# Eleven edits to the plan of a softmax-attention and spectral-filter kernel: first and last rounds, filler matmuls, first projection, last reciprocals

## The chip, the cores and the metric

The kernel runs on one core of one Trainium2 chip. The metric is the device time in microseconds of one execution, and the number to beat is the median of three runs. The engines named below are TensorE (PE, with its weight loads as PEld), VectorE (DVE), ScalarE (ACT), GpSimd (POOL) and SyncE (SP), which only issues transfers here.

## The reference, cut to what matters

A gate mixes two branches that read the same input `x` (2048 tokens of 448 channels): attention with 16 heads of 28 channels, and a filter in the Fourier domain.

```python
x = A_x                                                # [1, 2048, 448] bf16
g = sigmoid((x * gate_w).sum(-1, keepdims=True))
# a: attention
q, k, v = split_heads(x @ wqkv)                        # 16 heads, 28 channels each
p = softmax(q @ k.T * 28 ** -0.5)
a = merge_heads(p @ v) @ wo
# b: spectral filter
X = rfft2(x) * (w_r + 1j * w_i)
b = irfft2(X, s=(2048, 448))
return g * a + (1 - g) * b
```

## The kernel before, in words

The program is not written in the order in which it runs. Each method of the class `Kernel` describes operations (an engine, a planned duration, what they depend on, a key that is a due time, an earliest time `rel`), and the class `Sched` plays them through a small model of the core (`Sched.run`, L237). At each moment each engine takes the ready operation with the lowest key; transfers have a fixed planned latency. The order in which the model starts the operations is then emitted and fixed: on the chip every engine works its own list from the front, and waits where the front is not ready.

**Rounds.** Heads are worked in four groups `g` of four heads, tokens of the queries in four blocks `c` of 512. A round is one pair (g, c); there are 16 (`plan_steps`, L558), in the order (0,0), (0,1) to (3,3). In a round 16 tiles of 128 keys (`kt`) meet the block of queries for each of the four heads. One (kt, head) is a unit: a matmul with 32 rows (28 channels and the two norm terms) gives 128 keys x 512 queries of scores in PSUM, ACT takes the exponential, and four units of a tile, a quad, go into a PV matmul group that sums in the bank `pv`, with a ones column for the softmax denominators.

**Exponentials on ACT.** Units go in steps of three and two (`psA` of three banks, `psB` of two). L1143 evicts a step with one ACTIVATE into `ring`, which has 28 slots. A slot is taken again only when the PV matmul that read its last content is done, and PV quads run in a fixed order (`self.elems`).

**Exponentials on DVE and POOL.** `ND` says how many key tiles of a round ("d tiles") go another way: a dunit (a score matmul into one of two spare banks `bg`), a DVE instruction per head that turns the score into the bits of a bf16 power (L1099), and three more copies with a phase added (L1111, POOL or DVE), which PV multiplies with four scaled copies of V (`vd`), so a d tile costs four quads. `ND = [1] + [3] * 15`: key tile 15 in the first round, tiles 13 to 15 in the others. The d quads are spread through a round's list, the first one after three quads (where n % 4 == 0) or one.

**Two spare banks.** Everything else that TensorE does goes through the banks `bg`, an item at a time: transposing x (`x_block`), the projections of q and k (`proj_group`, L850: four matmul steps, two DVE instructions, a square sum `sq`, a row of norms `nrow` L885 and transfers of it into rows of q or k), of v (`v_block`), the gate (`gate_item`, L1001), the FFT stages (`background`, planned between `TA` 40 and `TB` 360 us) and the output tiles.

**Start.** `prologue` (L595) loads constants and the first 512 tokens, transposes them, and projects k and q of group 0 twice each: once into `psA`, squared by ACT (L708), and once into `psB`, onto which a matmul adds the norm row; DVE and ACT then evict `psB` (L719, L724, L728).

**After a round.** `normalise` (L1232) copies `pv` to SBUF, sends the denominators by DMA into a 128x16 tile, takes reciprocals (L1261), multiplies with the gate on POOL (L1262), goes through DRAM to spread them over partitions (`rsc`, `Rb`) and multiplies on POOL (L1272). For group 3 four output tiles can follow: eight matmul steps, k = 0 to 3 the spectral branch, 4 to 6 the earlier head groups, 7 group 3. After the last round there are no transfers: an fp32 matmul of 512 columns spreads the denominators, DVE takes the reciprocal of 128x512 (L1249) and multiplies, and `last_tile` (L1313) adds the last four output tiles in the banks that the scores have left.

**Filler.** Where the planned share of PE's time that was busy in the last 3.4 us (`HAMW`) is under `HAMF` = 0.7 and there is a gap, the planner puts a matmul of zeros into it, of the full array and up to 256 columns (`filler`, L800).

**Order of a group's projections.** `attention` (L1030) gives groups 1 to 3 due times a few us before the start of round 4g-1, all eight projections close together, and `v_block` after them.

Of the kernel before, what the change touches and what calls it, by code (L numbers as in the profile page):

```python
# [50 lines left out]
def fft_consts():  # L51
# [54 lines left out]
    for ri, B in enumerate((Br, Bi)):  # L106
# [8 lines left out]
       "sel4": (386, 32), "self": (418, 256)}  # L115
CSTN = 674


def small_consts():
# [26 lines left out]
    put32("self", self_)  # L146
    return m


class Op:  # L150
    __slots__ = ("lk", "eng", "dur", "emit", "deps", "key", "rel", "mode", "acq", "free", "lat",
                 "start", "end", "name", "step", "n")

    def __init__(self, eng, dur, emit, deps, key, rel, mode, acq, free, lat, name):
        self.eng, self.dur, self.emit = eng, dur, emit
        self.deps = [d for d in deps if d is not None]
        self.key, self.rel, self.mode = key, rel, mode
        self.acq, self.free, self.lat, self.name = acq, free, lat, name
        self.start = self.end = None
        self.step = None  # L160
        self.lk = eng == "POOL"

# [7 lines left out]
SWITCH = 0.1  # L170
HAMW, HAMF = 3.4, 0.7
DUE_P = 4.0
SWP = 1.0


class Sched:
# [60 lines left out]
    def run(self, nbg_tiles, dunits, dfree):  # L237
# [37 lines left out]
        def share(t):  # L275
            a = t - HAMW
            while pebusy and pebusy[0][1] <= a:
                pebusy.pop(0)
            return sum(e - max(s, a) for s, e in pebusy) / HAMW

        def fill(t):
# [17 lines left out]
            o = Op("PE", n / 2400.0, lambda: self.filler(target, n), (), 0.0, 0.0, "full", None, None, None, "fill")  # L299
            o.start = t + (SWITCH if mode not in (None, "full") else 0.0)  # L300
            o.end = o.start + o.dur
            order.append(o)
            pebusy.append((o.start, o.end))
# [3 lines left out]
        def finish(o, t0, dur):  # L307
            nonlocal left
            if o.eng == "PE":
                pebusy.append((t0, t0 + dur))  # L310
# [15 lines left out]
        while left:  # L326
            progress = False
            for e in engs:
                if free[e] > t + 1e-9:
                    continue  # L330
                best = None
                for o in pend[e]:
# [26 lines left out]
                if best is None:  # L359
                    if e == "PE" and t > 8.0:  # L360
                        f = fill(t)
                        if f:
                            free[e], mode = f, "full"
                            progress = True
# [58 lines left out]
class Kernel:  # L423
    ND = [1] + [3] * 15
    RING = 28
    T0 = 10.0
    TA, TB = 40.0, 360.0
# [25 lines left out]
    def alloc(self):  # L453
# [41 lines left out]
        self.gb3 = T([P, 512], BF16, "gb3")  # L495
# [62 lines left out]
    def plan_steps(self):  # L558
        self.groups = [(g, c) for g in range(4) for c in range(4)]
# [35 lines left out]
    def prologue(self):  # L595
        nc, sc = self.nc, self.sc
        K0 = -5000.0
        self.d_cst = self.dma(self.cst[:], nc.inline_tensor(small_consts(), name="ccst").ap(), (), K0, eng="AQ",
                              dur=0.1, lat=2.6)
# [89 lines left out]
        sv = self.c("svec").bitcast(F32)  # L689
        for wi, w in enumerate("kq"):  # L690
            b1 = [self.psA[:, 0, :], self.psA[:, 1, :]][wi]
            b2 = [self.psB[:, 0, :], self.psB[:, 1, :]][wi]
            first = {}
            for rnd, bank in ((0, b1), (1, b2)):
                ops = []
                for c in range(4):
                    n = 128 if c < 3 else 65

                    def f(c=c, n=n, w=w, bank=bank, rnd=rnd):
                        self.mm(bank, self.wpad[w, 0][0:n, c, :], self.xT[0][0:n, c, :], c == 0,  # L700
                                rnd == 0 and c == 3)
                    ops.append(self.pe(512, f, [self.xev[0, c]] + self.wready[w, 0] + ops[-1:],
                                       K0 + 20 + c * .1 + wi + 2 * rnd))
                first[rnd] = ops[-1]
# [4 lines left out]
            sq = self.act(0.65, fs, (first[0], tl, self.xev[0, 1]), K0 + 30 + wi)  # L709

            def fm(b2=b2, w=w, o=o):
                self.mm(b2, self.c("sel" + w), self.sq[:, o:o + 512], False, True)
            m = self.pe(512, fm, (sq, first[1]), K0 + 40 + wi)
            self.last_sqmm = m
            dst = self.k[0] if w == "k" else self.q[0]
            evs = []
            if w == "k":
                def fe(b2=b2, dst=dst):
                    self.pin(nc.vector.tensor_scalar(out=dst[:, 0:512], in0=b2, scalar1=sv, scalar2=None,  # L719
                                                     op0=ALU.mult))  # L720
                evs.append(self.dve(0.61, fe, (m,), K0 + 50))
            else:
                def fe1(b2=b2, dst=dst):
                    self.pin(nc.vector.tensor_scalar(out=dst[:, 0:272], in0=b2[:, 0:272], scalar1=sv,  # L724
                                                     scalar2=None, op0=ALU.mult))

                def fe2(b2=b2, dst=dst):
                    self.pin(nc.scalar.activation(out=dst[:, 272:512], in_=b2[:, 272:512], func=ACT.Copy, scale=sv))  # L728
                evs.append(self.dve(0.37, fe1, (m,), K0 + 51))
                evs.append(self.act(0.4, fe2, (m,), K0 + 51))  # L730
            (self.kev if w == "k" else self.qev)[0, 0] = evs
# [68 lines left out]
    def filler(self, bank, n):  # L800
        if bank is None:
            self.mm(self.pv[:, 0:n], self.zero[:, 0:P], self.zero[:, 0:n], False, False)
        elif bank < 0:
            self.mm(self.pv[:, 0:n], self.zero[:, 0:P], self.zero[:, 0:n], True, True)
        else:
            self.mm(self.bgt[bank][:, 0:n], self.zero[:, 0:P], self.zero[:, 0:n], True, True)
# [43 lines left out]
    def proj_group(self, w, g, blocks, due, rel):  # L850
# [5 lines left out]
        for j, b in enumerate(blocks):  # L856
            it = Item()
            dd = due - 8 + 5.0 * (j + 1) / nb
# [94 lines left out]
    def v_block(self, g, b, due, wop, rel=0.0):  # L953
# [23 lines left out]
        if b == 3:  # L977
            lo = 4 - min(len(self.dk[4 * g + c]) for c in range(4))
# [22 lines left out]
    def gate_item(self, due):  # L1001
# [5 lines left out]
        b = self.dve(0.16, lambda: self.pin(nc.vector.reciprocal(out=self.glog[:], in_=self.ge[:])), (a,), due)  # L1007
        b = self.dve(0.09, lambda: self.pin(nc.vector.tensor_copy(out=self.gg[:, 0:NT], in_=self.glog[:])), (b,), due)
# [18 lines left out]
        self.gb3d = self.dma(self.gb3[:], at([[0, P], [1, 512]], 12 * P), (s,), due + 2, lat=6.0)  # L1027


    def attention(self):  # L1030
# [15 lines left out]
        for g in range(1, 4):  # L1046
            d0 = ts[4 * g - 1]
            self.proj_group("k", g, [0, 1, 2, 3], d0 - 6.0, d0 - 60.0)
            self.proj_group("q", g, [0, 1, 2, 3], d0 - 2.0, d0 - 60.0)
            wop = self.w_block(g, [0, 1, 2, 3], d0 + 5, d0 - 15)  # L1050
            for b in range(4):
                self.v_block(g, b, d0 + 6 + 4.0 * b, wop, d0 - 15)
# [19 lines left out]
        for n, kt in dlist:  # L1072
# [14 lines left out]
            for s in range(4):  # L1087
# [7 lines left out]
                m.n = s  # L1095
                self.dunit_ops.append(m)
# [28 lines left out]
        for i, st in enumerate(self.steps):  # L1125
# [13 lines left out]
            m.step, m.n = i, [u[2] for u in st]  # L1139
            u0, ug = self.unit_slot[st[0]]  # L1140
# [91 lines left out]
    def normalise(self, n, last):  # L1232
# [8 lines left out]
        if n == 15:  # L1241
# [3 lines left out]
            m = self.pe(2048, lambda: self.mm(self.psB[:, 1, :], self.c("self").bitcast(F32), pvs[:], True, True),  # L1245
                        [ev, self.lastexp[1]], kk)
            a = self.dve(0.66, lambda: self.pin(nc.vector.tensor_tensor(out=pvs[:], in0=pvs[:], in1=self.gb3[:],
                                                                        op=ALU.mult)), (m, self.gb3d), kk, lk=True)
# [270 lines left out]
```

## Time and profile before

| | |
|---|---|
| median of 3 runs | 463.16 us (461.95 to 469.37) |
| the profiled execution | 463.34 us |
| its span, first to last instruction | 461.6 us |
| PE busy | 413.2 us, 90% |
| ACT busy | 390.1 us, 85% |
| DVE busy | 301.0 us, 65% |
| POOL busy | 261.0 us, 57% |
| mean granted TensorE clock | 0.948 |

The profiled execution is 1.7 us longer than its span, which is what lies around the first and the last instruction. A row of a timeline is: start, duration, engine, line, operation, output<-input with shapes, count, and in brackets how long the engine sat idle before it and what released it. A row of a table of stretches is: from and to, length, then the busy time of each engine with its count of instructions, the granted TensorE clock (1.00 is full), and the share and rate of the DMA engines.

### The profile page before, as it was taken

Reading aid. Unit: us, or ns where it says so; the run is one execution under the profiler, and the core shown is the slowest. Engines: PE = TensorE matmul, PEld = TensorE weight load, DVE = VectorE, ACT = ScalarE, POOL = GpSimd, SP = SyncE. Lnnn points to the kernel's source line nnn. Section 1 sums busy time; section 2 is a strip of 40 time slices with the busy share of each in tenths; the row PEclk is TensorE's granted clock in tenths of the full one; section 3 lists DMA queues with packets and bytes.
Section 4 is the critical chain, followed back from the end, with each engine's and each line's share of the span. In section 5 each row is a group of like instructions: output and inputs, shape, how many; then the busy total and the mean of one; then the engine's idle time right before and its main releaser. Section 6 shows DMA issues by size and latency. Waiting matters only on the chain.

```text
span 461.6 us, 11773 instructions
## 1 busy us (share of the span) xinstructions
PE 413.2 (90%) x4854; PEld 148.8 (32%) x4855; DVE 301.0 (65%) x492; ACT 390.1 (85%) x352; POOL 261.0 (57%) x230
## 2 busy tenths in 40 slices
PE   7889799989998898999889889799999899999894
PEld 5444221223342212223343223123333233333251
DVE  1558836776857847776867788366867776656325
ACT  2680667999999889999999899599999999999910
POOL 6825630673292387693296775398189592491910
PEclk9999855999999969999999999589999999999999
DMA  8210031101012321121112212002120221111101
GB/s 224 57 42 9 2 89 41 31 5 34 19 40 55 75 63 33 45 53 24 45 35 47 70 47 67 18 18 57 30 62 22 65 72 45 62 36 37 32 23 60
DMA packets 31586, 21.78 MB, mean 47 GB/s; under 512 B 16692, under 2 KB 29228, under 8 KB 31532
## 3 DMA queue, kind: packets, MB, share of 16 engines
q1 hardware_dynamic: 30140, 20.43, 17.2%
q8 instruction: 38, 0.62, 0.6%
q10 hardware_dynamic: 1392, 0.60, 0.5%
q14 instruction: 16, 0.13, 0.1%
HBM read 15.11 MB, written 1.97 MB: 37 GB/s over the span
## 4 chain that ended last, share of the span: by engine, by line
PE 38%; ACT 29%; DVE 9%; issue 8%; DMA 6%; SPq 6%; POOL 4%; ACTq 0%; POOLq 0%; DVEq 0%
ACT ring L1143 28%; PE bg L552 16%; PE pvb L552 10%; PE psA L552 7%; SPq L527 6%; PE psB L552 5%; POOL pd L1111 2%; DMA Rb<-rsc 2%; DMA X<-in_A_wqkv_dram 2%; DVE pd L1099 2%; DMA rsc<-rrg 1%; DVE pd L1111 1%; POOL q L1272 1%; DVE Rb L1249 1%; DVE vd L995 1%
## 5 line engine op out<-in xcount | busy, mean ns | idle before, releaser
L1143 ACT ACTIVATE ring<-psA 128x1536 bf16<-128x1536 f32 x168 | 260.4, 1550 | 17.6 <-PE psA L552 13.0
L1111 POOL TENSOR_SCALAR pd<-pd 128x2048 uint16<-128x2048 uint16 x105 | 197.4, 1902 | 80.3 <-DVE pd L1099 76.5
L1143 ACT ACTIVATE ring<-psB 128x1024 bf16<-128x1024 f32 x168 | 189.5, 1128 | 9.5 <-PE psB L552 8.9
L1099 DVE TENSOR_SCALAR pd<-bg 128x512 uint16<-128x512 f32 x184 | 122.4, 685 | 50.2 <-PE bg L552 38.3
L552 PEld LDWEIGHTS <-k 32*128 32x128 bf16 x1024 | 44.8, 91 | 151.3 <-issue 142.9
L552 PE MATMUL psA<-q,k 32*128 32x512 bf16 x504 | 70.2, 398 | 20.4 <-ACT ring L1143 16.5
L552 PE MATMUL pvb<-ring,vw 128*32 128x512 bf16 x840 | 84.7, 407 | 0.2
L552 PE MATMUL pvb<-pd,vd 128*32 128x512 bf16 x736 | 74.6, 401 | 4.9 <-POOL pd L1111 4.2
L552 PE MATMUL psB<-q,k 32*128 32x512 bf16 x336 | 70.4, 400 | 1.7 <-ACT ring L1143 1.2
L552 PE MATMUL bg<-q,k 32*128 32x512 bf16 x184 | 66.1, 396 | 2.8 <-DVE X L1366 1.4
L1272 POOL TENSOR_TENSOR q<-pvs,Rb 128x512 bf16<-128x512 f32 x15 | 19.2, 1282 | 32.8 <-DMA Rb<-rsc 17.2
L552 PEld LDWEIGHTS <-vw 128*32 128x32 bf16 x840 | 22.2, 97 | 26.6 <-issue 21.3
L552 PEld LDWEIGHTS <-vd 128*32 128x32 bf16 x736 | 19.9, 96 | 25.0 <-issue 20.1
L552 PEld LDWEIGHTS <-xT 128*32 128x32 bf16 (+3 forms) x512 | 20.1, 100 | 20.6 <-issue 17.7
L1111 DVE TENSOR_SCALAR pd<-pd 128x2048 uint16<-128x2048 uint16 x33 | 25.6, 798 | 0.2
L1423 DVE TENSOR_TENSOR t<-bg,Wg 128x450 bf16<-128x450 f32 x32 | 19.2, 618 | 7.2 <-PE bg L552 6.7
L552 PE MATMUL bg<-Bd,xT 128*32 128x450 bf16 (+1 forms) x256 | 20.4, 410 | 2.2 <-DVE X L1366 1.5
L864 DVE TENSOR_SCALAR q<-bg,cst 128x512 bf16<-128x512 f32 x15 | 11.3, 750 | 14.3 <-PE bg L552 14.3
L1309 DVE CAST fin<-bg 128x448 bf16<-128x448 f32 x12 | 7.5, 621 | 20.1 <-PE bg L552 20.1
L552 PE MATMUL bg<-xT,wpq 128*32 128x512 bf16 (+1 forms) x240 | 19.1, 399 | 0.0
L552 PE MATMUL bg<-xT,wpk 128*32 128x512 bf16 (+1 forms) x240 | 18.1, 387 | 0.5 <-DVE nrow L885 0.5
L1366 DVE CAST X<-bg 128x450 bf16<-128x450 f32 x16 | 9.9, 619 | 13.2 <-PE bg L552 13.2
(112 smaller groups left out, 366.1 us busy)
## 6 DMA issues: line engine op xcount, KB each, us to landing
Rb<-rsc SPq DMA_DIRECT2D x60, 64.0 KB
CS<-cCS SPq DMA_DIRECT2D x16, 192.0 KB
xtok<-Ab SPq DMA_DIRECT2D x16, 112.5 KB
Wg<-in_B_w_i_dram SPq DMA_DIRECT2D x64, 28.1 KB
V<-xtok SPq DMA_DIRECT2D x16, 112.5 KB
xtok<-in_A_x_dram SPq DMA_DIRECT2D x4, 448.0 KB
out_dram<-fin SPq DMA_DIRECT2D x12, 112.0 KB
Wg<-in_B_w_r_dram SPq DMA_DIRECT2D x32, 28.1 KB
```

Source lines behind the costliest of these rows:

```text
L527: self.pin(e.dma_start(out=out() if callable(out) else out, in_=in_() if callable(in_) else in_))
L552: self.pin(self.nc.tensor.matmul(out, lhsT=lhsT, rhs=rhs, start=start, stop=stop, **kw))
L864: self.pin(nc.vector.tensor_scalar(out=dst, in0=self.bgi(it), scalar1=self.sv, scalar2=None, op0=ALU.mult))
L995: self.pin(nc.vector.tensor_tensor(out=self.vd[g][:, f, :, :, 0:DH], in0=src, in1=wv, op=ALU.mult))
L1099: self.pin(nc.vector.tensor_scalar(out=ys[:, s, :].bitcast(U16), in0=self.bgi(it), scalar1=127 * UNITS, scalar2=0.0, op0=ALU.add, op1=ALU. ...
L1111: self.pin(e.tensor_scalar(out=fl(pds), in0=fl(ys), scalar1=float(PHASE[f]), scalar2=1.0, op0=ALU.add, op1=ALU.mult))
L1143: self.pin(nc.scalar.activation(out=self.ring[:, u0:u0 + len(st), :], in_=slot[:, 0:len(st), :], func=ACT.Exp, scale=LN2 / UNITS))
L1249: b = self.dve(0.66, lambda: self.pin(nc.vector.reciprocal(out=self.Rb[:], in_=self.psB[:, 1, :])), (m, self.rblast), kk)
L1272: e = self.pool(1.15, lambda: self.pin(nc.gpsimd.tensor_tensor(out=dst, in0=pvs[:], in1=self.Rb[:], op=ALU.mult)), ds, kk)
L1309: e = self.dve(0.55, lambda: self.pin(nc.vector.tensor_copy(out=fin[:], in_=self.bgi(it)[:, 0:D])), [ops[-1], self.fdma[t % 2]], key, free=it)
L1366: x1.append(self.dve(.54, lambda: self.pin(nc.vector.tensor_copy(out=self.X1[:, t, 0:F2], in_=self.bgi(it)[:, 0:F2])), ops[-1:] + pads, k, ...
L1423: self.pin(nc.vector.tensor_tensor(out=out[:], in0=self.bgi(it)[:, 0:F2].rearrange("p (a f) -> p a f", a=2), in1=free_dims(Wg[:], [[F, 2], ...
```

## The change

1. `ND[0]` goes from 1 to 0: in the first round all 16 key tiles go to ACT.
2. Filler: a matmul counts with a weight (`heat`), a quarter for each 32-row tile (dunit 0.25, score step 0.25 for each unit), 1 for all others; the bound `HAMF` goes from 0.7 to 0.5; a filler is four matmuls of 32 columns of weights each instead of one of 128.
3. A bank rule: an item that is no dunit may not take the last free `bg` bank while a ready dunit has a smaller key (`DUP`).
4. Constants are loaded in two parts (418 of 930 columns at the start; the rest, for the end, after planned time 60).
5. The first k and q are projected once. ACT squares the result, a matmul makes the norm rows in `psB`, ACT copies these to SBUF, and DVE adds them to the scaled projection.
6. The projections of groups 1 to 3 are spread: k and q get due times over a stretch from planned time 35, `ts[4]` or `ts[8]` to 16 us before the group's first round; v follows.
7. The order of the last eight rounds: (2,0), (2,1), (2,2), (3,0), (3,1), (3,2), (2,3), (3,3).
8. The rule "first d quad after three quads" holds for the first round of each group in that order.
9. After the last round: four small fp32 matmuls bring the denominators to a 128x16 tile, DVE takes the reciprocal and multiplies with the fp32 gate, copies it out to 128x512, four fp32 matmuls of 128 columns spread it into PSUM, and DVE multiplies.
10. The last output tiles: steps k = 0 to 6 get a late key (4000 + t instead of -30 + t), only k = 7 stays urgent.
11. The transfer of the gate's row (`gb3`) goes away.

```diff
-       "sel4": (386, 32), "self": (418, 256)}
-CSTN = 674
+       "sel4": (386, 32), "self": (418, 256), "idf": (674, 256)}
+CST1, CSTN = 418, 930
...
-HAMW, HAMF = 3.4, 0.7
+HAMW, HAMF = 3.4, 0.5
...
-            return sum(e - max(s, a) for s, e in pebusy) / HAMW
+            return sum((e - max(s, a)) * w for s, e, w in pebusy) / HAMW
...
+                        if ud is not None and o.name != "dunit" and len(bl) == 1 and ud < o.key + DUP:
+                            continue
...
-    ND = [1] + [3] * 15
+    ND = [0] + [3] * 15
+    PJE, PJV = 16.0, 16.0
...
-        self.groups = [(g, c) for g in range(4) for c in range(4)]
+        self.groups = ([(g, c) for g in range(2) for c in range(4)]
+                       + [(2, 0), (2, 1), (2, 2), (3, 0), (3, 1), (3, 2), (2, 3), (3, 3)])
...
+        for wi, w in enumerate("kq"):
+            b1, b2, o = self.psA[:, wi, :], self.psB[:, wi, :], 512 * wi
+            m = self.pe(512, lambda b2=b2, w=w, o=o: self.mm(b2, self.c("sel" + w), self.sq[:, o:o + 512], True, True),
+                        (sqs[w],), K0 + 40 + wi)
...
+            def fn(nr=nr, b2=b2):
+                self.pin(nc.scalar.copy(out=nr[:], in_=b2))
+            nn = self.act(0.5, fn, (m,), K0 + 45 + wi)
...
+                self.pin(nc.vector.scalar_tensor_tensor(out=dst[:, 0:512], in0=b1, scalar=sv, in1=nr[:],
+                                                        op0=ALU.mult, op1=ALU.add))
...
-            self.mm(self.bgt[bank][:, 0:n], self.zero[:, 0:P], self.zero[:, 0:n], True, True)
+        out = self.pv if bank is None or bank < 0 else self.bgt[bank]
+        self.mm4(out[:, 0:n], self.zero[:, 0:P], self.zero[:, 0:n], bank is not None, bank is not None)
...
-            dd = due - 8 + 5.0 * (j + 1) / nb
+            dd = due - 3 - spread * (nb - 1 - j) / nb
...
-            d0 = ts[4 * g - 1]
-            self.proj_group("k", g, [0, 1, 2, 3], d0 - 6.0, d0 - 60.0)
-            self.proj_group("q", g, [0, 1, 2, 3], d0 - 2.0, d0 - 60.0)
+            b0 = ts[self.fr[g]] - self.PJE
+            a0 = [0, 35.0, ts[4], ts[8]][g]
+            m0 = (a0 + b0) / 2
+            self.proj_group("k", g, [0, 1, 2, 3], m0, a0 - 10.0, m0 - a0)
+            self.proj_group("q", g, [0, 1, 2, 3], b0, a0 - 10.0, b0 - m0)
...
-            lo = 3 if n % 4 == 0 else 1
+            lo = 3 if n == self.fr[self.groups[n][0]] else 1
...
+                m.heat = 0.25
...
+            m.heat = 0.25 * len(st)
...
-            m = self.pe(2048, lambda: self.mm(self.psB[:, 1, :], self.c("self").bitcast(F32), pvs[:], True, True),
-                        [ev, self.lastexp[1]], kk)
...
-            b = self.dve(0.66, lambda: self.pin(nc.vector.reciprocal(out=self.Rb[:], in_=self.psB[:, 1, :])),
-                         (m, self.rblast), kk)
...
+                ms.append(self.pe(0, lambda j=j: self.mm(bank[:, 4 * j:4 * j + 4], pvs[:, 128 * j:128 * j + 128],
+                                                         self.c("self").bitcast(F32)[:, 0:128:32], True, True),
...
+            a = self.dve(0.2, lambda: self.pin(nc.vector.reciprocal(out=r[:], in_=bank[:, 0:16])), ms[-1:], kk)
...
+                ms2.append(self.pe(0, lambda j=j: self.mm(bank[:, 128 * j:128 * j + 128], self.Rx[:, j, :],
+                                                          self.c("idf").bitcast(F32), True, True),
...
+            x = self.dve(0.6, lambda: self.pin(nc.vector.tensor_copy(
+                out=self.Rx[:].rearrange("p j (s n) -> p j s n", n=32),
+                in_=free_dims(r2[:], [[4, 4], [1, 4], [0, 32]]))), (b,), kk)
...
+            e = self.dve(0.61, lambda: self.pin(nc.vector.tensor_tensor(out=dst, in0=pvs[:], in1=bank, op=ALU.mult)),
+                         ms2[-1:], kk)
...
-            o = self.pe(448, f, self.out_dep(t, k) + ops[-1:] + (self.lastexp if k == 0 else []), -30.0 + t, mode="col")
+            o = self.pe(448, f, self.out_dep(t, k) + ops[-1:] + (self.lastexp if k == 0 else []),
+                        -30.0 + t if k == 7 else 4000.0 + t, mode="col")
```

More of the change, by code (lines that the diff above doesn't have):

```diff
@@ L331, in run @@
                 best = None
+                ud = None
+                if e == "PE":
+                    for o in pend[e]:
+                        if o.name == "dunit" and rdy[o] <= t + 1e-9 and (ud is None or o.key < ud):
+                            ud = o.key
                 for o in pend[e]:
@@ L362, in run @@
                         if f:
-                            free[e], mode = f, "full"
+                            free[e], mode = f, "col"
                             progress = True
@@ L977, in v_block @@
         if b == 3:
[L978 removed]
+            lo = 4 - min(len(self.dk[self.nof[g, c]]) for c in range(4))
         vr = [wop[1]]
```

101 lines of the change are left out of this document (47 added, 54 removed).

## The prediction

> **What bounds the kernel now.** I read the page first (busy shares, then the 40 slices), then what ACT waited for, then the timelines of ACT and PE at the places where ACT's row is low.
>
> ```profile
> span 461.6 us, 11773 instructions
> PE 413.2 (90%) x4854; PEld 148.8 (32%) x4855; DVE 301.0 (65%) x492; ACT 390.1 (85%) x352; POOL 261.0 (57%) x230
> ACT  2680667999999889999999899599999999999910
> PEclk9999855999999969999999999589999999999999
> ```
>
> ACT's row is 9 almost everywhere between slices 7 and 38: the exponentials bound the middle. They are low at both ends, nil in slice 3, and low where the clock row reads 5 or 6. So I split the time into four terms: the head up to the first exponential, the exponentials back to back, ACT's waits between them, the tail.
>
> ```profile
> 15.32 1.45 ACT L1143 ACTIVATE ring<-psA 128x1536 bf16<-128x1536 f32 x1 [1.02 <-PE psA L552]
> ...
> 17.57 1.46 ACT L1143 ACTIVATE ring<-psA 128x1536 bf16<-128x1536 f32 x1
> ...
> 23.38 1.45 ACT L1143 ACTIVATE ring<-psA 128x1536 bf16<-128x1536 f32 x1 [1.10 <-PE psA L552]
> ...
> 31.56 1.12 ACT L1143 ACTIVATE ring<-psB 128x1024 bf16<-128x1024 f32 x1
> 39.21 0.18 ACT L933 ACTIVATE w<-bg 128x16 f32<-128x16 bf16 x1 [6.53 <-PE bg L555]
> 45.97 0.21 ACT L1003 ACTIVATE ge<-glog 128x16 f32<-128x16 f32 x1 [6.58 <-DVE glog L972]
> 48.27 1.45 ACT L1143 ACTIVATE ring<-psA 128x1536 bf16<-128x1536 f32 x1 [2.08 <-PE pvb L552]
> ...
> 438.79 1.03 ACT L1143 ACTIVATE ring<-psB 128x1024 bf16<-128x1024 f32 x1
> ```
>
> Head: 15.3. A pair of steps (five units) starts every 2.25 us (15.32 to 17.57), 0.45 a unit. The last exponential ends at 439.8, so the phase lasts 424.5 and the tail 461.6 - 439.8 = 21.8. ACT's waits between exponentials, by releaser:
>
> ```profile
> ACT ring L1143 <- PE psA L552: 13.0, 18, 1.6
> ACT ring L1143 <- PE psB L552: 8.9, 12, 2.8
> ACT ring L1143 <- PE bg L552: 2.9, 4, 1.1
> ACT ring L1143 <- PE pvb L552: 2.1, 1, 2.1
> ```
>
> Together 26.9, with the 6.53 and 6.58 of the two small ACTIVATEs above 40.0, less the 1.0 before the first exponential: 39.0. So 840 units take 424.5 - 39.0 = 385.5. Of the 39.0, 15.2 is one hole: nothing is evicted between 32.7 (31.56 + 1.12) and 48.27. By then 14 steps or 35 units are done, the ring holds 28, and only the first pair of quads (8 units) has been read: the second pair holds the first d quad of key tile 15, which waits for the last block of keys, its dunits and `vd`. The hole ends on a PV matmul. The other 23.8 lie mainly where the clock is halved:
>
> ```profile
> 50.00:80.00 30.00, 27.90 (x218) 6.18 (x214) 16.10 (x27) 20.40 (x18) 8.53 (x6) 0.60 0.21 50
> 160.00:180.00 20.00, 18.97 (x181) 4.83 (x179) 11.37 (x20) 17.59 (x16) 12.95 (x7) 0.74 0.20 52
> 280.00:310.00 30.00, 26.91 (x266) 7.42 (x265) 18.27 (x28) 23.75 (x21) 16.16 (x15) 0.77 0.14 34
> ```
>
> ACT is the fourth number with a count: idle 9.6 of the 30 us from 50, 2.4 of the 20 from 160, 6.2 of the 30 from 280, 18.2 in all. That leaves 23.8 - 18.2 = 5.6, of which 1.1 is the wait at 23.38.
>
> **First round on ACT (edits 1, 8).** It adds four units, 4 x 0.45 = 1.8 us, and takes four dunits, four DVE evictions, three phase copies and three PV quads net out of the first 50 us. The hole of 15.2 goes, since no PV quad of the first round waits for a d tile any more. What is late next is the second round's first d quad, which needs the same `vd` and the second block of queries. Its last DVE eviction before:
>
> ```profile
> 54.54 1.29 DVE L1099 TENSOR_SCALAR pd<-bg 128x512 uint16<-128x512 f32 x2 [0.27 <-PE bg L552]
> ```
>
> So at 55.8 even if nothing gets earlier, while ACT reaches round two at about 15 + 1.1 + 64 x 0.45 = 45 and has 28 slots, 12.6 us, in hand. So I count the hole as gone, and bound what comes in its place between 0 and 5 us: DVE must now do in 30 us, beside running exponentials, the projections that it did in the hole.
>
> **Filler, weights, bank rule (2, 3).** No row prices four-column fillers. There are 76 in this phase (55 and 21, rows below); if each held a score up by its pitch of 0.11 us (four in 0.61, each 0.28 long, so (0.61 - 0.28) / 3) that would be 8 us, if all lie in gaps, 0. They are put only where the plan has a gap and PE's matmuls leave 10% of the span open, so I take 0. The bank rule holds another item back by one dunit's eviction at most (0.65 by the row above, two in 1.29), and the spectral items that yield have until planned time 360: 0. What the fillers are worth is the clock:
>
> ```profile
> L552 PE MATMUL pvb<-zero x55: 230/282/394, 26.6 to 347.0; 128*128 128x256 bf16 x49, 128*128 128x128 bf16 x2, 128*128 128x192 bf16 x2, 128*128 128x224 bf16 x1
> L552 PE MATMUL bg<-zero x21: 272/273/283, 286.8 to 457.7; 128*128 128x256 bf16 x21
> ...
> 436.96 0.61 PE L552 MATMUL bg<-zero 128*128 128x256 bf16 x4
> ...
> 46.00:54.00 8.00, 5.10 (x66) 1.95 (x66) 7.96 (x13) 4.00 (x4) 5.62 (x3) 1.00 0.00 0
> 162.00:164.00 2.00, 1.46 (x11) 0.47 (x7) 1.78 (x4) 2.00 (x3) 0.21 (x1) 1.00 0.39 99
> 288.00:291.00 3.00, 0.50 (x5) 0.10 (x2) 0.00 (x0) 1.93 (x2) 3.00 (x3) 0.90 0.00 0
> ...
> 287.89 1.26 POOL L1272 TENSOR_TENSOR q<-pvs,Rb 128x512 bf16<-128x512 f32 x1 [5.13 <-DMA Rb<-rsc]
> ...
> 291.07 0.62 PE L552 MATMUL pvb<-pd,vd 128*32 128x512 bf16 x4 [2.56 <-POOL pd L1111]
> ```
>
> Each fall follows thin work. Before the first, DVE is full (7.96 of 8) and PE busy 5.10 of 8; the change lightens exactly that place. The second, at 164, comes with PE at work, mostly 32-row tiles: the weighted count sees it, the old one did not. The third is a surprise to any plan: POOL waits 5.13 for `Rb`, its next phase copy is late, PE stands 2.56. I take that one fall like the later two remains somewhere, (2.4 + 6.2) / 2 = 4.3, and bound it by 0 and 18.2.
>
> The Trainium skill, "TensorE: Matmul & The Clock Gate", section "Why this matters for your kernels", has the clock fall back after a matmul gap of about 3 us. The row of 288 to 291 agrees (2.56 idle), that of 162 to 164 does not (0.54 idle of 2, and it fell). By that rule alone the weighting would buy nothing at 164, and the sum would be 2.4 higher.
>
> **Single projection (4, 5).** It takes eight 512-column matmuls off PE and ACT's q eviction, and adds two ACT copies, which I price like the squares.
>
> ```profile
> 11.10 0.60 ACT L708 ACTIVATE sq<-psA 128x512 bf16<-128x512 f32 x1 [0.46 <-PE psA L552]
> ...
> 12.42 0.60 PE L552 MATMUL psB<-sq,cst 128*128 128x512 bf16 x2
> ...
> 13.05 0.75 DVE L719 TENSOR_SCALAR k<-psB,cst 128x512 bf16<-128x512 f32 x1 [4.35 <-DMA X<-in_A_wqkv_dram]
> ...
> 14.33 0.50 DVE L724 TENSOR_SCALAR q<-psB,cst 128x272 bf16<-128x272 f32 x1 [0.53 <-ACT q L728]
> ```
>
> The squares end at 11.7. Then: k copy 0.6, q norm matmul 0.4 (two take 0.60, the second begins 0.2 later), q copy 0.6, q add 0.75, and hops of 0.06 make 14.3, against 14.83 now, the end of the DVE part of q. First exponential at 14.8; bounds 14 (k and q overlap) and 15.8. The first wait, for the second key block (23.38), does not move, so it grows by the half microsecond: 1.6. The smaller constant load, the second one on SP's queue in mid-kernel and the missing `gb3` transfer touch queues on which no exponential waits here: 0.
>
> **Spread projections, order of rounds (6, 7).** The same instructions, moved. The SP and POOL queues see the same transfers in another order; of the 4.5 us of small waits left (5.6 - 1.1) I keep all, between 0 and 8. Group 3 starts a round earlier, but its keys' buffer is free from round 8, three rounds ahead. The gain of the order is in the tail: tiles 8 to 11 can be finished during rounds 14 and 15.
>
> **Tail (9, 10).** Now:
>
> ```profile
> 439.89 0.93 PE L552 MATMUL psA<-Bd,X 113*32 113x448 bf16 x16
> 440.65 0.74 PE L552 MATMUL psA<-wo,q 128*32 128x448 bf16 x12
> 441.22 0.93 PE L552 MATMUL psA<-Bd,X 113*32 113x448 bf16 x16
> ...
> 448.45 0.60 PE L552 MATMUL pvb<-ring,vw 128*32 128x512 bf16 x8
> 449.86 1.12 PE L552 MATMUL psB<-pvs,cst 128*128 128x512 f32 x2 [0.61 <-DVE pvs L1243]
> 451.63 3.35 DVE L1249 RECIPROCAL Rb<-psB 128x512 f32<-128x512 f32 x1
> 455.01 0.69 DVE L1251 TENSOR_TENSOR q<-pvs,Rb 128x512 bf16<-128x512 f32 x1
> ...
> L1261 DVE RECIPROCAL rr<-rs 128x16 f32<-128x16 f32 x15 | 3.6, 242 | 2.8 <-DMA rs<-pvs 2.8
> ```
>
> From 439.9 output steps run for 8.3 us ahead of the last PV group (ends 449.05); then 0.8 copy, 1.8 spreading, 3.35 reciprocal, 0.7 multiply, and 5.9 from 455.7 for the last step, the evictions and the transfer. After: PV first, its end about 1.0 after the last exponential; copy 0.8; four small matmuls; reciprocal 0.3; gate 0.25; copy out 0.7; four spreading matmuls; multiply 0.85; then 5.9. The small matmuls have no row: between 0.5 and 2.4, I take 1.3, near the 1.12 of the fp32 one; the spreading ones between 1.0 and 2.8, I take 1.8 (the same columns plus exposed weight loads). Sum 12.9. The steps k = 0 to 6 of four tiles (439.89 to 441.22 is one tile, 5.3 us of PE in all) no longer stand ahead, but only some 4 of it fits into the gaps: plus 1.3. Tail 14.2; bounds 12 and 16.7.
>
> **Sum.** Head 14.8 + exponentials 385.5 + 1.8 + waits (1.6 + 4.5 + 4.3 = 10.4) + tail 14.2 = 426.7, plus the 1.7 around the span: 428. That is against this execution's 463.3, which is the median (463.16) within 0.1.
>
> **Rivals.** (A) The waits stay: the hole goes, but the clock falls as long as before and DVE and the two banks, full early on, hold round two up. Waits 23.8 + 5, rest as above: 447. For it: 7.96 of 8 us of DVE before the first fall, and falls like the third that no filler sees. Against: PE gets scores and PV at the place where it was thin. The page's rule above belongs here.
>
> (B) The clock never falls and the waits shrink to the first one and some 2 us: 3.6, total 422. Against: one late `Rb` among 15 is enough.
>
> (C) The hole only moves: the second round's d quads stall the ring as the first did, 15.2 again with the old clock stretches: 14.8 + 387.3 + 39 + 14.2 + 1.7 = 457, no change to speak of. Against: three times as many key tiles pass before it.
>
> (D) Slower: the halved clock. In the 30 us from 50 ACT lost 9.6, of which by the mean clock some 24 halved: 0.40 lost per halved microsecond. If the narrow fillers do not hold the clock, it takes (463.3 - 428 + 9.3) / 0.40, about 112 us halved beyond what I counted, to be 2% slower. Against: the whole middle runs at 1.00 on narrow tiles.
>
> **Chances.** Mine (waits 6 to 18, 424 to 436) 0.55; A (436 to 454) 0.21; B 0.11; C 0.08; D 0.05. 2% is about what a measurement of this kernel can tell from no change: faster holds mine, A and B, 0.87; same C, 0.08; slower 0.05. The range reaches from 416 (B with no wait and a tail of 12) to 450 (A's upper part left out, with C and D).
>
> **What would show it.** Hole: no ACT wait over 3 us between 30 and 50. Head: first exponential before 15.3. Clock: the three fives of the clock row gone or fewer. Tail: last exponential to end about 14, no 3.35 reciprocal, the last PV group within 1.5 us of the last exponential. I am wrong if ACT stalls on PV in the second round, or if the clock row shows more fives.

## The result, and the profile after

| | before | after | predicted |
|---|---|---|---|
| median | 462.56 us (4 runs) | 436.63 us (4 runs, 435.51 to 438.8) | 428 (416 to 450) |
| ratio to before | | 0.9486, 95% interval 0.9384 to 0.9587 | |
| profiled execution, its span | 463.34, 461.6 | 438.8, 437.0 | |
| mean granted TensorE clock | 0.948 | 0.978 | |

Faster by 5.1%, inside the range. Medians take in all runs and ratios leave out those slowed by a low clock, from one of which the profile of before stems, so the two spans lie a little further apart than the ratio.

The page of the changed kernel, the same lines as before:

```profile
span 437.0 us, 11982 instructions
...
PE 390.3 (89%) x4956; PEld 145.9 (33%) x4957; DVE 295.3 (68%) x489; ACT 391.1 (89%) x355; POOL 254.9 (58%) x227
...
ACT  2888999998979999979997899999999999898970
...
PEclk9998999999999999988998989999999999999999
```

ACT is never nil in the middle now, and the clock row has no digit under 8. ACT's timeline, start, duration and in brackets the wait:

```profile
14.74 1.45 ACT L1150 ACTIVATE ring<-psA 128x1536 bf16<-128x1536 f32 x1 [1.27 <-PE psA L563]
...
23.66 1.45 ACT L1150 ACTIVATE ring<-psA 128x1536 bf16<-128x1536 f32 x1 [1.81 <-PE psA L563]
...
107.99 1.45 ACT L1150 ACTIVATE ring<-psA 128x1536 bf16<-128x1536 f32 x1 [1.30 <-PE pvb L563]
115.98 1.45 ACT L1150 ACTIVATE ring<-psA 128x1536 bf16<-128x1536 f32 x1 [0.86 <-PE pvb L563]
125.34 1.45 ACT L1150 ACTIVATE ring<-psA 128x1536 bf16<-128x1536 f32 x1 [2.48 <-PE pvb L563]
...
192.59 1.45 ACT L1150 ACTIVATE ring<-psA 128x1536 bf16<-128x1536 f32 x1 [1.35 <-PE psA L563]
...
236.93 1.02 ACT L1150 ACTIVATE ring<-psB 128x1024 bf16<-128x1024 f32 x1 [1.55 <-PE psB L563]
...
250.86 1.02 ACT L1150 ACTIVATE ring<-psB 128x1024 bf16<-128x1024 f32 x1 [1.12 <-PE pvb L563]
...
422.50 0.75 ACT L1150 ACTIVATE ring<-psB 128x512 bf16<-128x512 f32 x1
```

The hole of 32.7 to 48.3 is gone. What is new is an exponential that waits on PV, which means a full ring. By releaser (total us, times, longest):

```profile
ACT ring L1150 <- PE pvb L563: 11.4, 10, 2.5
ACT ring L1150 <- PE psA L563: 7.8, 9, 1.8
ACT ring L1150 <- PE bg L563: 2.8, 4, 1.1
ACT ring L1150 <- PE psB L563: 1.8, 2, 1.6
```

PV held ACT once for 2.1 us before, and at the end of the hole only; now ten times. PE does not stand still meanwhile. In the longest of these waits, from 122.87 to 125.34, it is busy for 2.44 of 2.47 us:

```profile
122.87:125.34 2.47, 2.44 (x46) 1.46 (x46) 1.22 (x2) 0.00 (x0) 2.47 (x2) 1.00 0.00 0
...
123.24 0.57 PE L563 MATMUL bg<-Bd,xT 128*32 128x450 bf16 x8
123.74 0.97 PE L563 MATMUL bg<-wvr,xT 128*128 128x112 bf16 x16
124.64 0.40 PE L563 MATMUL pvb<-pd,vd 128*32 128x512 bf16 x4
124.87 0.39 PE L563 MATMUL pvb<-ring,vw 128*32 128x512 bf16 x4
```

Matmuls of the spectral branch (`Bd`) and the projections of v (`wvr`) stand in PE's list ahead of the PV quad that frees the slots. In none of the ten waits, nor in the 3 us before each, does PE idle for a phase copy; once, ahead of 250.86, it idles 1.6 us for a square sum on DVE. So PV comes late mainly by its place in the order, whatever made the planner put it there.

Stretches with a reduced clock (the fourth number with a count is ACT, the last but two the clock):

```profile
190.00:200.00 10.00, 7.58 (x79) 1.98 (x74) 4.94 (x8) 6.24 (x7) 10.00 (x9) 0.66 0.14 33
230.00:242.00 12.00, 9.48 (x117) 2.78 (x115) 6.33 (x11) 9.36 (x9) 8.63 (x6) 0.86 0.25 63
250.00:256.00 6.00, 6.00 (x73) 1.61 (x69) 3.94 (x8) 4.05 (x4) 1.09 (x2) 0.72 0.12 24
```

ACT idles 3.8 + 2.6 + 1.9 = 8.3 us there, against 18.2 in the three stretches before. Cut to the stretches in which the clock is halved (three of before, then four of after), they add up to 47.8 us before and 17.0 after:

```profile
54.90:78.80 23.90, 23.52 (x175) 5.00 (x178) 11.17 (x19) 16.73 (x15) 5.87 (x4) 0.50 0.26 61
164.10:174.30 10.20, 10.20 (x78) 1.95 (x76) 3.31 (x6) 7.89 (x7) 10.20 (x6) 0.50 0.17 49
290.40:304.10 13.70, 13.03 (x100) 2.52 (x99) 7.16 (x11) 8.08 (x7) 4.99 (x5) 0.50 0.06 17
...
32.30:35.70 3.40, 3.40 (x31) 0.75 (x28) 0.75 (x1) 2.95 (x3) 0.00 (x0) 0.50 0.07 20
192.70:199.50 6.80, 6.05 (x53) 1.46 (x56) 3.19 (x6) 4.39 (x4) 6.80 (x6) 0.50 0.11 31
237.10:240.50 3.40, 3.40 (x35) 0.70 (x31) 1.27 (x3) 2.65 (x3) 2.72 (x2) 0.50 0.25 74
250.80:254.20 3.40, 3.40 (x28) 0.70 (x24) 1.75 (x4) 2.46 (x3) 1.09 (x2) 0.51 0.09 17
```

And the tail:

```profile
424.44 0.40 PE L563 MATMUL pvb<-pd,vd 128*32 128x512 bf16 x4 [0.31 <-POOL pd L1117]
424.66 0.62 PE L563 MATMUL pvb<-ring,vw 128*32 128x512 bf16 x8
...
425.35 0.69 DVE L1250 COPY pvs<-pvb 128x512 f32<-128x512 f32 x1 [7.98 <-PE pvb L563]
...
426.34 1.06 PE L563 MATMUL psB<-cst,pvs 128*128 128x4 f32 x8
...
427.50 0.26 DVE L1259 RECIPROCAL rs<-psB 128x16 f32<-128x16 f32 x1 [1.47 <-PE psB L563]
...
428.07 0.43 DVE L1268 COPY Rb<-rr 128x512 f32<-128x512 f32 x1
...
428.77 1.16 PE L563 MATMUL psB<-cst,Rb 128*128 128x128 f32 x8
...
429.96 0.69 DVE L1273 TENSOR_TENSOR q<-pvs,psB 128x512 bf16<-128x512 f32 x1 [1.47 <-PE psB L563]
```

PV ends 2.0 us after the last exponential (9.2 before), and the reciprocal of 3.35 is one of 0.26.

Four terms make the span of every profile: the start of the first exponential (head), the sum of the gaps between exponentials (waits), the rest of that phase (exponentials), and from the last exponential to the end (tail). The experiments stand in the table with their medians; each profile is one execution.

| kernel | head | exponentials | waits | of them on PV | tail | span | median us (runs) |
|---|---|---|---|---|---|---|---|
| before | 15.3 | 384.9 | 39.6 | 2.1 | 21.8 | 461.6 | 462.56 (4) |
| predicted | 14.8 | 387.3 | 10.4 | | 14.2 | 426.7 | 428 |
| after | 14.7 | 385.6 | 22.9 | 11.4 | 13.8 | 437.0 | 436.63 (4) |
| after again (a0) | 14.2 | 385.5 | 25.2 | 14.3 | 13.7 | 438.6 | 437.63 (5) |
| e1, d tile in round one | 14.5 | 382.9 | 36.7 | 7.5 | 14.3 | 448.4 | 450.91 (4) |
| b1, before, none in round one | 15.6 | 385.3 | 30.5 | 7.1 | 22.2 | 453.6 | 455.90 (10) |
| e4, old tail | 14.8 | 385.7 | 23.0 | 11.4 | 18.6 | 442.1 | 442.90 (4) |
| e5, old order | 14.4 | 385.9 | 24.1 | 7.3 | 21.5 | 445.9 | 449.83 (4) |
| e2, old filler | 15.2 | 385.9 | 31.2 | 12.3 | 14.2 | 446.5 | 448.75 (4) |
| e3, no filler | 17.2 | 387.0 | 41.5 | 15.7 | 16.0 | 461.7 | 462.31 (4) |
| e6, old due times | 17.9 | 386.5 | 38.4 | 17.9 | 13.8 | 456.7 | 456.94 (10) |
| e7, no bank rule | 14.5 | 386.2 | 41.7 | 22.4 | 13.9 | 456.3 | 458.31 (10) |
| e8, SP issue at its price | 14.4 | 384.8 | 17.9 | 6.7 | 13.9 | 431.0 | 432.96 (4) |
| e9, dunits early | 14.8 | 385.9 | 33.6 | 15.5 | 13.9 | 448.1 | 448.52 (4) |
| c1, due times 0.3 later | 14.5 | 386.8 | 34.0 | 14.0 | 13.8 | 449.1 | 454.19 (4) |

The exponentials hardly differ, 382.9 to 387.0. The tail follows the edits, but for e3's, which has 4.0 us of halved clock ahead of its last steps (445.7 to 449.7). The head is 14.2 to 15.6, but for e3 and e6, whose clock was halved at the start. The waits are where the kernels differ, from 17.9 to 41.7. Between the profiles of before and after, 24.6 us apart, the head gives 0.6, the hole 15.6, the tail 8.0 and the other waits 1.1 (24.0 to 22.9), and the exponentials take 0.7 more.

### The profile page after: what moved, and what is told of

It reads as the page before. It is cut to its first block, busy times and chain, and to the rows that moved or that the text cites. A ratio compares the mean times of both kernels' runs of the same rounds, so it can differ in the third digit from the quotient of the medians.

```text
span 437.0 us, 11982 instructions
## 1 busy us (share of the span) xinstructions
PE 390.3 (89%) x4956; PEld 145.9 (33%) x4957; DVE 295.3 (68%) x489; ACT 391.1 (89%) x355; POOL 254.9 (58%) x227
## 3 DMA queue, kind: packets, MB, share of 16 engines
q1 hardware_dynamic: 30140, 20.43, 17.2%
## 4 chain that ended last, share of the span: by engine, by line
ACT 42%; PE 26%; issue 10%; DVE 8%; DMA 6%; POOL 5%; SPq 2%; POOLq 1%; ACTq 0%; DVEq 0%
ACT ring L1150 42%; PE bg L563 10%; PE pvb L563 7%; PE psA L563 5%; PE psB L563 4%; POOL pd L1117 4%; DMA rsc<-rrg 2%; DVE pd L1105 2%; DMA Rb<-rsc 2%; SPq L538 2%; DVE pd L1117 1%; DMA X<-in_A_wqkv_dram 1%; DVE k L867 1%; DVE sq L872 1%; POOL q L1294 1%
## 5 line engine op out<-in xcount | busy, mean ns | idle before, releaser
L1150 ACT ACTIVATE ring<-psA 128x1536 bf16<-128x1536 f32 x169 | 263.6, 1560 | 16.7 <-PE pvb L563 8.8
L1117 POOL TENSOR_SCALAR pd<-pd 128x2048 uint16<-128x2048 uint16 x102 | 191.9, 1901 | 84.9 <-DVE pd L1105 56.0
L1150 ACT ACTIVATE ring<-psB 128x1024 bf16<-128x1024 f32 (+1 forms) x169 | 191.5, 1133 | 7.4 <-PE bg L563 2.8
L1105 DVE TENSOR_SCALAR pd<-bg 128x512 uint16<-128x512 f32 x180 | 120.0, 686 | 45.6 <-PE bg L563 38.6
L563 PE MATMUL psA<-q,k 32*128 32x512 bf16 x507 | 67.4, 387 | 20.2 <-ACT ring L1150 16.7
L563 PE MATMUL pvb<-ring,vw 128*32 128x512 bf16 x844 | 82.0, 391 | 0.4 <-DVE pvs L1280 0.4
L563 PE MATMUL pvb<-pd,vd 128*32 128x512 bf16 x720 | 71.6, 392 | 2.1 <-POOL pd L1117 2.1
L563 PE MATMUL psB<-q,k 32*128 32x512 bf16 x337 | 68.3, 389 | 3.5 <-ACT ring L1150 3.0
L563 PEld LDWEIGHTS <-vd 128*32 128x32 bf16 x720 | 19.6, 96 | 21.7 <-issue 18.2
L563 PEld LDWEIGHTS <-xT 128*32 128x32 bf16 (+3 forms) x512 | 18.9, 96 | 16.9 <-issue 14.7
L563 PE MATMUL bg<-Bd,xT 128*32 128x450 bf16 (+1 forms) x256 | 17.5, 358 | 0.0
L1389 DVE CAST X<-bg 128x450 bf16<-128x450 f32 x16 | 10.0, 626 | 10.4 <-PE bg L563 8.3
L1451 POOL TENSOR_TENSOR Z<-t 128x225 bf16<-128x225 bf16 x16 | 10.0, 623 | 11.4 <-DVE t L1446 11.4
```

Of the source, the lines that this page charges most:

```text
L563: self.pin(self.nc.tensor.matmul(out, lhsT=lhsT, rhs=rhs, start=start, stop=stop, **kw))
L1105: self.pin(nc.vector.tensor_scalar(out=ys[:, s, :].bitcast(U16), in0=self.bgi(it), scalar1=127 * UNITS, scalar2=0.0, op0=ALU.add, op1=ALU. ...
L1117: self.pin(e.tensor_scalar(out=fl(pds), in0=fl(ys), scalar1=float(PHASE[f]), scalar2=1.0, op0=ALU.add, op1=ALU.mult))
L1150: self.pin(nc.scalar.activation(out=self.ring[:, u0:u0 + len(st), :], in_=slot[:, 0:len(st), :], func=ACT.Exp, scale=LN2 / UNITS))
L1389: x1.append(self.dve(.54, lambda: self.pin(nc.vector.tensor_copy(out=self.X1[:, t, 0:F2], in_=self.bgi(it)[:, 0:F2])), ops[-1:] + pads, k, ...
L1451: z1 = self.pool(.55, lambda t12=t12, Z=Z: self.pin(nc.gpsimd.tensor_tensor(out=Z[:, 0, :], in0=t12[:, 0, :], in1=t12[:, 1, :], op=ALU.sub ...
```

## The experiments

Four groups of kernels ran, on three chips, each beside before, whose medians were 460.37 (a0, e1, b1, e4), 457.22 (e2, e3, e5, e6), 458.83 (e7, e8, e9) and 460.08 us (c1). A difference to a0 across groups carries up to these 3 us.

**The changed kernel again.** 

> The changed kernel again, as the yardstick of this group: about 436 us, ACT's waits between exponentials about 22, tail about 14. Every theory expects the same of it.

437.63 us, ratio 0.9583 (0.9405 to 0.976). The waits move by 2.3 between two executions of one order.

**The hole, from both sides.** First a d tile back into the first round of the changed kernel:

```diff
-    ND = [0] + [3] * 15
+    ND = [1] + [3] * 15
```

> The changed kernel with one d tile in the first round again (ND[0] = 1). Theory 1 (the hole was a stall of the ring and its removal is a net gain): the hole of about 15 us comes back around 30 to 50 and the time rises by 15.2 - 1.8 = 13, to about 449. Rival (the hole was where the background work got done, and without it that work is paid later): the hole comes back but the waits later shrink by as much, so the time rises by less than 5.

```profile
32.19 1.12 ACT L1150 ACTIVATE ring<-psB 128x1024 bf16<-128x1024 f32 x1
38.07 0.18 ACT L936 ACTIVATE w<-bg 128x16 f32<-128x16 bf16 x1 [4.76 <-PE bg L566]
45.62 0.22 ACT L1006 ACTIVATE ge<-glog 128x16 f32<-128x16 f32 x1 [7.37 <-DVE glog L975]
47.90 1.45 ACT L1150 ACTIVATE ring<-psA 128x1536 bf16<-128x1536 f32 x1 [2.06 <-PE pvb L563]
```

450.91 us, ratio 0.99 (0.9775 to 1.0025): 13.3 more than a0. The hole is back where it was, 33.3 to 47.9, 14.6 long, and the other waits are 36.7 - 14.6 = 22.1, as in the changed kernel. Then the same line alone, in the kernel before:

```diff
-    ND = [1] + [3] * 15
+    ND = [0] + [3] * 15
```

> The kernel before with ND[0] = 0 and nothing else. Theory 1: the hole goes and the time falls by 13, to about 449 to 450. Rival (work paid later): the hole goes, but new waits of 8 us or more appear after it, and the time falls by less than 5.

455.9 us by the median, 4.5 less, but ratio 1.005 (1.0011 to 1.009): no gain. The hole goes, and the other waits grow from 39.6 - 15.6 = 24 to 30.5, although the profile of before is the one with the lower clock (0.948 against 0.961). My 13 us held in one plan and not in the other.

**The tail.** The old reciprocal chain and urgent keys:

```diff
+            m = self.pe(2048, lambda: self.mm(self.psB[:, 1, :], self.c("self").bitcast(F32), pvs[:], True, True),
...
+            b = self.dve(0.66, lambda: self.pin(nc.vector.reciprocal(out=self.Rb[:], in_=self.psB[:, 1, :])),
...
-                        -30.0 + t if k == 7 else 4000.0 + t, mode="col")
+                        -30.0 + t, mode="col")
```

> The changed kernel with the old end of the last round (one fp32 matmul of 512 columns, the reciprocal of 128x512, the multiply with the gate's row) and the old urgent keys for all steps of the last tiles. Theory 2: the output steps stand ahead of the last PV group again (5.3 us) and the long reciprocal is back (3.35 against about 1.3 for the short chain plus more spreading), so the tail is 13.8 + 5 to 7 = 19 to 21 and the time about 442 to 443. Rival (the order of the rounds alone shortened the tail, since tiles 8 to 11 are done before): tail under 16 and less than 2.5 us more.

442.9 us, ratio 0.9703 (0.9602 to 0.9804), 5.3 more than a0; tail 18.6, 4.9 more, all else equal. It takes back edits 9, 10 and 11 together (the `gb3` transfer is back as well). In the two traces PE's matmuls, by the tiles they read and write, stand in the same order up to 424.4 us. So this price, of the three together, stands, but for about 0.6 us: the last steps ran at a halved clock here (1.31 us for 12 matmuls that took 0.75 before). The order of the rounds:

```diff
-        self.groups = ([(g, c) for g in range(2) for c in range(4)]
-                       + [(2, 0), (2, 1), (2, 2), (3, 0), (3, 1), (3, 2), (2, 3), (3, 3)])
+        self.groups = [(g, c) for g in range(4) for c in range(4)]
```

> The changed kernel with the rounds in the old order. My prediction had its gain in the tail: four output tiles (8 to 11) of about 1.5 us of PE each move behind the last exponential, so a tail longer by 2 to 5 and a time of 439 to 442. Rival: those tiles fit into the last round anyway, tail and time within 1.5.

449.83 us, ratio 0.9871 (0.9787 to 0.9954), and the tail 21.5: 7.7 more, where I had said 2 to 5. Four output tiles stand in the tail again, two ahead of PV (PE from 425.3 to 428.6) and two between the short chain and the last steps. The two need each other: with the new order alone the tail is 18.6, with the new chain and keys alone 21.5, with neither 21.8 to 22.2 (before and b1, which lack the other edits too), with both 13.7 to 13.8.

**Filler.** The old one, of the full array and unweighted:

```diff
-HAMW, HAMF = 3.4, 0.5
+HAMW, HAMF = 3.4, 0.7
...
-                m.heat = 0.25
...
-            m.heat = 0.25 * len(st)
```

> The changed kernel with the old filler: full-array matmuls of zeros, every matmul counted with weight 1, bound 0.7. Theory 3 (the weighted count keeps the clock up): more of the clock row under 9, granted clock under 0.97 instead of 0.98 to 0.99, ACT's waits up by 4 to 10 us, time 440 to 446. Rival (falls come from waits that no plan sees): clock and time within 0.01 and 2.5 us of the changed kernel.

448.75 us, ratio 0.986 (0.9793 to 0.9928), clocks 0.962 to 0.973 in four runs, waits 31.2. None at all:

```diff
-                    if e == "PE" and t > 8.0:
+                    if e == "PE" and t > 1e9:
```

> The changed kernel without any filler after the start. If fillers hold the clock at all: granted clock under 0.95, several stretches of 10 to 25 us halved, 445 to 460. If they do not: within 2.5 us of the changed kernel, and 46 fillers of four matmuls less on PE.

462.31 us, ratio 1.0148 (1.0055 to 1.0242), clocks 0.922 to 0.933, waits 41.5. No other kernel has all its runs so low, and in e3's profile the clock is halved for 67.4 us before the tail, against 17.0 and 20.4 in the two profiles of the changed kernel and at most 47.8 in the others. So fillers hold the clock; but the order of the other matmuls differs here too, and the 24.7 us against a0 need not be the fillers' price alone.

**Due times and bank rule.** The old due times:

```diff
-            b0 = ts[self.fr[g]] - self.PJE
...
+            d0 = ts[self.fr[g] - 1]
+            self.proj_group("k", g, [0, 1, 2, 3], d0 - 6.0, d0 - 60.0)
+            self.proj_group("q", g, [0, 1, 2, 3], d0 - 2.0, d0 - 60.0)
```

> The changed kernel with the old due times of the projections of groups 1 to 3, eight close together. Prediction: no effect on ACT's waits (within 2 us). Rival a (bunched projections hold PE and the two banks, and PV and dunits come late): waits up by 3 to 8 us. Rival b (the spread itself, which puts projections of group 1 into 90 to 130 us, causes the new waits on PV there): those waits, 4.6 us between 107 and 126, go away and the time falls by 2 to 5.

456.94 us, ratio 1.0023 (0.9974 to 1.0071), 19.3 more than a0, beyond every expectation. The bank rule:

```diff
-                        if ud is not None and o.name != "dunit" and len(bl) == 1 and ud < o.key + DUP:
-                            continue
```

> The changed kernel without the bank rule (a background item may take the last free bank although a dunit waits). Prediction: the rule costs and brings nothing, within 2 us of 437. Rival (the rule is what feeds the d tiles in time once the hole is gone): ACT's waits on PV up from 11 to over 18, time 443 or more.

458.31 us, ratio 1.0029 (0.9969 to 1.0088), 20.7 more. Its waits on PV are 22.4, one of them 8.8, as the rival said.

**A neutral edit.** By now five undone edits (e1, e2, e5, e6, e7) had cost 13.3 + 11.1 + 12.2 + 19.3 + 20.7 = 76.6 us against a0, three times what the whole change brings. So I moved the planned start of the first round by 0.3 us:

```diff
-    T0 = 10.0
+    T0 = 10.3
```

> A neutral edit of the changed kernel: the planned start of the first round, from which the due times follow, is 10.3 instead of 10.0 us. Nothing is added or taken away, only ties and near ties in the plan fall otherwise. If the single undos measured their own effect (5 to 21 us each), this one stays within 2 us of 437. Rival (any edit throws the plan's order anew, and the changed kernel's order is a good draw): it loses 4 us or more too, and then no single undo under that size proves its own mechanism; what is then left to trust is what shows in its own place in the trace (the hole, the tail).

454.19 us against 460.08 of before; the best runs of the two are 450.89 and 451.0. The edit adds and removes no step of the computation, and it costs 16.6 us against a0 (14.0 between the best runs, 450.89 and 436.86): its waits are 34.0 instead of 25.2, the surplus between 200 and 400 us, and its clocks are 0.937 to 0.973 where those of a0 are 0.965 to 0.988. In the two traces PE's lists of matmuls, by the tiles they read and write, agree for the first 1,046 of 4,956, to 99.7 us, and after that they differ, in 2,112 lines of a comparison; c1 has 60 narrow filler matmuls more. The rival holds: this edit, which only shifts the plan, dealt the order of what follows anew. It is one draw; how far others would go is not known. With this draw the whole change brings 5.9 us by the medians and next to nothing between the best runs, so the 5.1% above belong to the change together with the order that it happened to get.

**Two tries at the new waits.** SP's issues in the plan at the price of the traces:

```diff
-    def dma(self, out, in_, deps, key, eng="SP", rel=0.0, dur=0.15, lat=None, name="dma"):
+    def dma(self, out, in_, deps, key, eng="SP", rel=0.0, dur=0.43, lat=None, name="dma"):
...
-            ds.append(self.dma(o, i, [ev] + e1s, due - 2.5, dur=0.12))
+            ds.append(self.dma(o, i, [ev] + e1s, due - 2.5, dur=0.5))
```

> The changed kernel with the plan told the time of a DMA issue on SP that the traces show (0.43 us, 0.5 for the norm rows, instead of 0.15 and 0.12; four Rb issues took 1.71 us). Theory 4 (ACT's new waits on PV come from phase copies that stand behind the multiply of the normalisation on POOL, which the plan expects too early): those waits fall from 11 to under 6 and the time to 430 to 434. Rival (they come from d tiles that the plan itself starts late): no less PV waits, time within 3 us of 437.

432.96 us, ratio 0.9483 (0.9428 to 0.9538), the best median of all, below both kernels; its ratio's interval overlaps that of the changed kernel. Waits on PV fell to 6.7, as theory 4 had it (to under 6, it said). POOL's wait before the multiply was shorter too; the rows are a0, e8 and e9, the next run:

```profile
POOL q L1294 <- DMA Rb<-rsc: 31.7, 8, 12.0
POOL q L1294 <- DMA Rb<-rsc: 23.4, 7, 7.9
POOL q L1294 <- DMA Rb<-rsc: 18.3, 7, 6.7
```

But it was shortest in e9, whose waits on PV are 15.5, so the two do not go together; in the changed kernel PE idles for no phase copy while ACT waits on PV; and 5 us is less than a neutral edit moves. The cause stays open. Dunits earlier:

```diff
-DUE_P = 4.0
+DUE_P = 8.0
```

> The changed kernel with the dunits planned 8 instead of 4 us ahead of their first PV quad (DUE_P). Theory 5 (the plan starts d tiles too late): ACT's waits on PV fall from 11 to under 6, time 429 to 434. Rival (the eight buffers of phase copies and the two banks hold them back anyway): PV waits stay at 9 to 13 and the time within 3 us of 437. Theory 4 expects PV waits to stay as well, since POOL's place in line does not change.

448.52 us, ratio 0.9795 (0.9708 to 0.9882), waits on PV 15.5. Theory 5 is not borne out; the rival's "within 3 us" is not either.

## Why the prediction was right or wrong

**Hole: right, and only as part of this plan.** There is no wait over 2 us between 24 and 107, round two was not held up, and e1 brings the hole back in its place, 14.6 long. That e1's time rises by 13.3 us, beside my 15.2 - 1.8 = 13.4, is in part luck, since a neutral edit moves more than that. In b1 other waits took all of it; "I count the hole as gone" was true, that its 13 us would stay gained was not to be read from it.

**Head: right in number** (14.8 forecast; 14.7, a0 14.2). Its cause is not shown: no run undoes the single projection or the split constants (edits 4, 5), and kernels that begin with the same order of matmuls have heads from 14.2 to 15.2 where the clock was full, beside 15.3 before.

**Tail: right in sum** (13.8 to 14.2). PV ended 2.0 after the last exponential, not 1.0, since it waited for a phase copy, which POOL ended at 424.4. The small matmuls took 1.06 and 1.16, where I had 1.3 and 1.8, and the copy out 0.43, not 0.7. What I did not see is how much the edits need each other: undoing the order of the rounds alone costs 7.7 of the tail, where the whole forecast gain was 21.8 - 14.2 = 7.6, and the new chain and keys save 4.9 in the new order, next to nothing (21.8 to 21.5) in the old one.

**Waits: the step that failed.** "Waits (1.6 + 4.5 + 4.3 = 10.4)" measured 22.9: this one term is 12.5 off and the sum 10.3 (437.0 - 426.7). The first wait was right (1.96). The clock's share is 8.3 by the stretches that I had forecast it from, instead of 4.3, two falls' worth; but 1.35 and 1.55 of it are waits that ended as the clock fell (at 192.7 and 237.1), and 0.9 is the end of a wait on PV. Inside the halved stretches, waits on PV left out, ACT loses 4.5 us (15.1 before), close to my 4.3. What else is left, without the first wait, is 22.9 - 11.4 - 4.5 - 2.0 = 5.0, beside my 4.5. So the term that I did not have at all is the whole miss: 11.4 us of PV late for a full ring, in rounds four and on, not in round two where I had looked. The step was to carry over the small waits of the old order ("I keep all, between 0 and 8") when projections and rounds moved; the new order has waits of its own, 5.0 + 11.4. 436.6 lies just past the upper edge of the case I called mine (436), in rival A's band, but not by A's mechanism: the clock fell less than before (1 - 0.978 against 1 - 0.948) and the early rounds ran free. That the time fell inside my range is in part luck of the order: c1, with the same edits and a shifted start, takes 454, outside of it.

**Bank rule, due times: "0" not shown.** I priced them at nothing. Undone, each costs some 20 us, but a neutral edit costs 16.6, and one draw does not bound the swing. What they are worth apart from the order that they happen to give stays open; many neutral draws with and without each would tell.

**Filler weights.** Fillers hold the clock (e3). The 2.56 us of idle at 288 to 291 is short of the 3 us beside which the prediction sets it, so that row agrees only roughly. That the weighted count is the better one is not shown: e2 loses 11.1, less than c1. The changed kernel has fewer fillers than before, 46 (184 narrow matmuls) instead of 76.

**Rivals.** B, C and D did not come; C's place (the second round) shows nothing. That the gain would shrink because any order has waits of its own was in none of them, and it is the main finding.

## What to carry to other kernels

Where a planner fixes the order, split the span into terms that keep their place (here head, exponentials, tail) and one that does not (waits), and price an edit by its place; for the rest, run neutral edits first: a single undo that moves the time by no more than they do (16.6 us here, from one) proves nothing of its own mechanism. A price that is argued only from one trace's waits is a price in that order. A plan that is told a wrong duration (0.15 for a DMA issue of 0.43) is worth mending before its order is tuned, though e8's gain of 5 us does not prove it.

## What the runs showed of the hardware that I had not expected

The mean granted clock goes with the spread of a fixed order: of 26 runs of before beside the first two groups the slowest, 467.51 us, had a mean clock of 0.930, and one of the fastest, 452.3, had 0.984; that is 15 us for 0.054 of mean clock. Within the rounds every stretch at half clock lasts 3.4 us or a multiple of it: 3.4, 6.8, 3.4, 3.4 in the changed kernel, 23.9, 10.2, 13.7 before.

The clock can fall at the start too. In e3 PE waited 1.68 us for the first transposed block, in e6 2.31; the clock was halved from 9.4 and 8.3 us on, and the first exponential came at 17.2 and 17.9. Up to there their order of matmuls is that of the changed kernel, whose profile has a wait of 1.57 there and the full clock (last row), so that wait alone does not show what makes it fall.

```profile
6.00:12.00 6.00, 3.67 (x20) 1.51 (x19) 2.37 (x6) 0.74 (x2) 2.60 (x7) 0.78 1.06 303
12.00:18.00 6.00, 4.62 (x34) 3.31 (x34) 3.35 (x6) 3.02 (x5) 5.24 (x18) 0.65 0.15 33
...
6.00:12.00 6.00, 3.24 (x26) 1.77 (x25) 2.45 (x8) 1.84 (x4) 2.15 (x6) 1.00 1.00 285
```

The Trainium skill, "TensorE: Matmul & The Clock Gate", section "What's actually happening", says that the window over which activity is measured runs freely and does not start with the kernel. That one order falls at different places in two executions agrees with it, as far as these runs can show it: at 32.3 us in the changed kernel's profile, first at 102.7 in a0's.

An fp32 matmul of 4 columns costs about what one of 128 does: four of each, eight records, took 1.06 us and 1.16 us in the tail above.
